# FFN's first half: GpSimd's second weight sum moved behind the next block's input-weight remainder

## The chip, the cores and the metric

The kernel runs on one core of a Trainium2 chip. The metric is the device time of one execution in microseconds. Its engines are TensorE (matrix products; in the profile PE, and PEld for its weight loads), VectorE (DVE), ScalarE (ACT), GpSimd (POOL) and SyncE (SP, which issues most transfers). Each engine works through its own queue in order and waits on semaphores for the others.

## The reference, cut to what matters

Three stages in a row: attention restricted to clusters of queries and keys, a feed-forward network (FFN) with a leaky activation, and a mixture of eight experts. The change is in the second:

```python
def _moe_ref(x, w_in, w_out, alpha) -> np.ndarray:
    h = x @ w_in
    g = np.maximum(h, 0.0) + alpha * np.minimum(h, 0.0)
    return (g @ w_out).astype(np.float32)
```

x is 1536 tokens x 512, w_in 512 x 2048, w_out 2048 x 512. The two weight matrices are given as 8-byte floating-point numbers, so the kernel has to make 4-byte ones of them.

## The kernel before

The FFN cuts the hidden width of 2048 into NF = 16 blocks f of 128 and the tokens into two halves gi of 768. The first half (gi = 0) runs through all 16 blocks, then the second half does. Block f's weights are 128 x 512 numbers of w_in and as many of w_out.

Each 4-byte operand is split into a rounded part and a remainder (`wh` and `wl` of the weights, `gh` and `gl` of the activations, `xh` and `xl` of x), and each product is made of three: high x high, and high x low both ways.

TensorE's order in a block of the first half: `product(c, i)` of line 672 for c = 0, 1 (two runs of 384 tokens) and i = 0, 1, 2: `wh` with xh, `wh` with xl, `wl` with xh, four matmuls each (line 677); then `second(0, f - 1)` (line 719), the previous block's activations times w_out, 18 matmuls (line 726).

After the three products of each c the activation follows: VectorE makes `gm` in two instructions from the PSUM tile h (lines 702 and 703), ScalarE rounds it to `gh` (line 705), VectorE subtracts to `gl` (line 707). Then `after(c)` (line 796) is issued:

- after c = 0: `split(f + 1, 0)` and `split(f, 1)`: the input weights of the next block and the output weights of this one. In each, ScalarE rounds to `wh` (line 648) and GpSimd subtracts to `wl` (line 649).
- after c = 1: `convert(f + 2)` (line 630): the 8-byte weights of block f + 2 become 4-byte ones in two halves, input weights and output weights. `word` (line 560) is a generator: ScalarE makes two operands (lines 569 and 570), VectorE takes three instructions (lines 571, 573, 575) in place in a tile `ct`, of which there are two buffers, and GpSimd adds at last (line 577). `convert` steps both halves in turn, so that each engine gets the first half's instruction and then the second's.

GpSimd's order in a block is therefore: the sum of the input weights, the sum of the output weights (both of line 577, issued by the block before), the subtraction for the next block's input weights, the subtraction for this block's output weights (both of line 649). In the texts below these four are A, B, X and Y. Blocks 2 to 13 convert; blocks 14 and 15 have nothing left to convert. Conversion of block 3 is issued ahead of block 2 (line 792), beside the end of the attention's normalisation on GpSimd (lines 412 to 415).

All order is that of the program's text; no planner moves anything.

Of the kernel before, what the change touches and what calls it, by code (L numbers as in the profile page):

```python
# [543 lines left out]
class Convert:  # L544
# [10 lines left out]
    def load(self, f):  # L555
        raw = self.slot(f)
        self.nc.sync.dma_start(out=raw[:, :DM].rearrange("p (k n) w -> p k (n w)", k=DM // P), in_=self.w_in[:, :, f])
        self.nc.sync.dma_start(out=raw[:, DM:].rearrange("p n w -> p (n w)"), in_=self.w_out[:, f])
# [53 lines left out]
def ffn(tc, A, cst, xs, xp, y1d, R, cv, W32, fw, ps_h, spare, more):  # L612
# [17 lines left out]
    def convert(f):  # L630

        if f < NF:
            gs = [cv.word(f, slice(q * DM, (q + 1) * DM), ck.tile([P, DM], I32, tag="ct", name="ct")) for q in range(2)]
            for _ in range(4):
                for g in gs:
                    next(g, None)

    ws, gs, over = {}, {}, {}

    def split(f, o, eng, gi=0):  # L640

        if o == 1 and gi == 1 and NF - TAIL <= f < NF - 2:
            wh, wl = over["xl"].pop(0), over["xl"].pop(0)
        else:
            wh = fw.tile([P, DM], F32R, tag=f"wh{o}", name=f"wh{o}")
            wl = fw.tile([P, DM], F32R, tag=f"wl{o}", name=f"wl{o}")
        w = W32(f)[:, o * DM:(o + 1) * DM]
        nc.scalar.copy(wh, w)
        eng.tensor_tensor(out=wl, in0=w, in1=wh.bitcast(F32), op=ALU.subtract)  # L649
        ws[f, o] = (wh, wl)  # L650
# [7 lines left out]
    def hidden(gi, f, eng, after, between=lambda: None):  # L658
        for _ in hiddens(gi, f, eng, after, between):
            pass  # L660

    def hiddens(gi, f, eng, after=lambda c: None, between=lambda: None, act=False):
# [17 lines left out]
        for c in range(2):  # L680
# [29 lines left out]
            if not act or f + c == 2:  # L710
                pay()
            after(c)
            if c == 1:
                gs[f] = (gh, gl)
# [4 lines left out]
    def second(gi, f, ns=range(3), ts=range(GT)):  # L719
        wh, wl = ws[f, 1]  # L720
        gh, gl = gs[f]
        for n, (a, w) in enumerate(((gh, wh), (gh, wl), (gl, wh))):
            for t in ts if n in ns else ():
                if f == 0 and n == 0:
                    ys[gi * GT + t] = ps_y.tile([P, DM], F32, tag="y", name="y")
                nc.tensor.matmul(ys[gi * GT + t], lhsT=a[:, t * P:(t + 1) * P], rhs=w,  # L726
                                 start=(f == 0 and n == 0), stop=(gi == 0 and f == NF - 1 and n == 2))
        if ns[-1] == 2 and ts[-1] == GT - 1:
            del ws[f, 1], gs[f]
# [60 lines left out]
    for f in (4, 5, 6):  # L790
        load(f)
    convert(3)
    second(0, 0)
    for f in range(2, NF):

        def after(c):
            if c == 0:
                split((f + 1) % NF, 0, nc.gpsimd)
                split(f, 1, nc.gpsimd)
            else:  # L800
                convert(f + 2)

        hidden(0, f, nc.vector, after)
        if f + 5 < NF:
            load(f + 5)
        second(0, f - 1)
# [742 lines left out]
def kernel(ctx, tc, A):  # L1549
# [164 lines left out]
    def begin():  # L1714
        ps_h = c2.enter_context(tc.tile_pool(name="ps_h", bufs=2, space=PSUM, side="right", reuse_waits="tile"))
        fw = c0.enter_context(tc.tile_pool(name="ffw", bufs=2, side="right", reuse_waits="tile"))
        return ffn(tc, A, cst, xs, xp, y1d, R, cv, lambda f: w32[f], fw, ps_h, spare, lambda *a: got.append(a) if a else more())
# [108 lines left out]
```

## Time and profile before

| | us |
|---|---|
| median of 3 runs | 718.74 |
| lowest, highest | 717.54, 721.0 |
| the profiled execution, device time | 718.92 |
| its span, first to last instruction | 717.1 |
| mean granted TensorE clock | 0.994 |
| busy: TensorE, weight loads | 699.9, 625.8 |
| busy: VectorE, ScalarE, GpSimd | 568.2, 472.1, 381.9 |

The profile is one execution. A page gives sums; views of the trace give groups of instructions, waits, and the instructions in order of time. Times in them are from the span's start, and the loop of the first half runs from about 263 to 385 us. Matmuls are pipelined, so that their busy times overlap and starts tell more than durations. In the order of time, instructions of one line that follow each other without a gap may stand merged as one row with their count (x2).

### The profile page before, as it was taken

How to read it: one execution, taken by the hardware profiler on the slowest of the kernel's cores; microseconds unless marked ns; L12 is line 12 of the kernel's file. 1: busy time of each engine (PE TensorE's matmuls, PEld its weight loads, DVE VectorE, ACT ScalarE, POOL GpSimd, SP SyncE). 2: the span in 40 equal slices, each digit the busy share in tenths (PEclk: the TensorE clock that was granted, in tenths of full speed). 3: DMA queues.
4: the chain of work that ended last, by engine and by line, in shares of the span. 5: the costliest groups of instructions: out<-in, count | busy, mean ns of one | idle time of the engine just before them, and what ended most of it. 6: DMA issues, size and time to landing. Idle time of an engine off the chain costs nothing.

```text
span 717.1 us, 11778 instructions
## 1 busy us (share of the span) xinstructions
PE 699.9 (98%) x4111; PEld 625.8 (87%) x4111; DVE 568.2 (79%) x1114; ACT 472.1 (66%) x905; POOL 381.9 (53%) x339
## 2 busy tenths in 40 slices
PE   8999999999999999999999999999999999999995
PEld 5998989989999899888889999999888989898884
DVE  6989988898989878788784989976468888785651
ACT  6889788888889954554545655556645867574640
POOL 4659779697896386666662000001025888884201
PEclk9999999999999999999999999999999999999998
DMA  7867666676765133333203600026444999996000
GB/s 204 213 160 177 133 166 157 156 173 127 169 164 123 41 115 122 133 138 136 119 1 122 188 0 1 1 64 202 147 149 139 385 367 320 353 352 262 33 10 25
DMA packets 43904, 108.42 MB, mean 151 GB/s; under 512 B 8698, under 2 KB 24522, under 8 KB 38464
## 3 DMA queue, kind: packets, MB, share of 16 engines
q1 hardware_dynamic: 36768, 67.03, 34.4%
q0 software_dynamic: 7072, 40.60, 15.3%
q8 instruction: 34, 0.56, 0.3%
q14 instruction: 30, 0.25, 0.1%
HBM read 74.78 MB, written 10.10 MB: 118 GB/s over the span
## 4 chain that ended last, share of the span: by engine, by line
PE 66%; DVE 8%; DMA 8%; ACT 6%; POOL 6%; issue 5%; POOLq 0%; SPq 0%; ACTq 0%; DVEq 0%
PE h L677 18%; PE y L726 16%; DMA raw<-in_wall_dram,wi 7%; PE yo L1210 5%; PE pt L342 4%; PE hw L1263 4%; PE h L1210 3%; PE s L308 2%; PE px L360 2%; DVE nm L324 2%; PE y L736 2%; ACT e L331 2%; PE s L311 2%; DVE etl L345 2%; PE px L362 2%
## 5 line engine op out<-in xcount | busy, mean ns | idle before, releaser
L345 DVE TENSOR_TENSOR etl<-pt,eth 128x384 fp32r<-128x384 f32 x192 | 101.9, 549 | 19.6 <-ACT eth L344 18.4
L344 ACT CAST eth<-pt 128x384 fp32r<-128x384 f32 x192 | 90.9, 485 | 19.4 <-PE pt L342 19.4
L1177 POOL DMA_INDIRECT xg<-y1d,gi x16 | 27.8, 1738 | 130.5 <-DVE gi L1026 113.8
L342 PE MATMUL pt<-ident,e 128*128 128x128 f32 x576 | 93.8, 272 | 0.3 <-ACT e L331 0.3
L331 ACT ACTIVATE e<-s,nm 128x768 f32<-128x768 f32 x96 | 87.4, 910 | 6.4 <-DVE nm L324 5.6
L324 DVE TENSOR_REDUCE nm<-s 128x1 f32<-128x768 f32 x96 | 90.5, 943 | 0.9 <-PE s L311 0.8
L705 ACT CAST gh<-gm 128x384 fp32r<-128x384 f32 x60 | 30.8, 513 | 81.8 <-DVE gm L703 58.5
L342 PEld LDWEIGHTS pt<-ident,e 128*128 128x128 f32 x576 | 73.6, 140 | 7.0 <-ACT e L331 0.6
L707 DVE TENSOR_TENSOR gl<-gm,gh 128x384 fp32r<-128x384 f32 x60 | 49.4, 824 | 25.7 <-ACT gh L705 25.7
L360 PE MATMUL px<-etl,vh 128*64 128x384 f32 (+1 forms) x192 | 65.5, 368 | 1.5 <-DVE etl L345 1.3
L308 PE MATMUL s<-AB 128*128 128x384 f32 x192 | 57.5, 381 | 2.5 <-ACT e L331 2.1
L577 POOL TENSOR_TENSOR pre<-ct,pre 128x512 int32<-128x512 int32 x26 | 37.2, 1451 | 35.8 <-DVE ct L575 35.8
L677 PE MATMUL h<-xh,wh 128*128 128x384 f32 x256 | 55.6, 338 | 0.6 <-DVE gm L700 0.4
L677 PE MATMUL h<-xh,wl 128*128 128x384 f32 x256 | 56.0, 339 | 0.0
L677 PE MATMUL h<-xl,wh 128*128 128x384 f32 x256 | 55.0, 336 | 0.0
L362 PE MATMUL px<-eth,vh 128*128 128x384 f32 x160 | 54.0, 337 | 0.0
L1545 DVE TENSOR_TENSOR wl<-raw,wh 128x2048 fp32r<-128x2048 f32 (+2 forms) x26 | 44.5, 1717 | 11.7 <-ACT wh L1541 11.7
L311 PE MATMUL s<-CD 128*128 128x384 f32 x192 | 49.3, 338 | 1.0 <-DVE CD L439 1.0
L677 PEld LDWEIGHTS h<-xh,wh 128*128 128x128 f32 x256 | 45.5, 188 | 3.3 <-DVE gm L700 0.5
L677 PEld LDWEIGHTS h<-xh,wl 128*128 128x128 f32 x256 | 44.6, 188 | 2.7 <-POOL wl L649 2.6
L677 PEld LDWEIGHTS h<-xl,wh 128*128 128x128 f32 x256 | 45.7, 188 | 0.0
L1541 ACT CAST wh<-raw 128x2048 fp32r<-128x2048 f32 (+2 forms) x26 | 37.4, 1444 | 10.6 <-PE yo L1210 10.6
(357 smaller groups left out, 1816.8 us busy)
## 6 DMA issues: line engine op xcount, KB each, us to landing
AB<-RL SPq DMA_DIRECT2D x31, 384.0 KB, 5.3
raw<-in_w_in_dram SPq DMA_DIRECT2D x16, 512.0 KB, 4.0
raw<-in_w_out_dram SPq DMA_DIRECT2D x16, 512.0 KB, 4.7
raw<-in_wall_dram SPq DMA_DIRECT2D x8, 1024.0 KB, 8.2
Tp<-in_qkT_dram SPq DMA_DIRECT2D x16, 384.0 KB, 4.1
CD<-RL SPq DMA_DIRECT2D x15, 384.0 KB, 6.9
raw<-in_wall_dram POOLq DMA_DIRECT2D x4, 1024.0 KB, 11.8
vt<-in_v_dram SPq DMA_DIRECT2D x8, 384.0 KB, 6.3
```

What stands on the lines that cost most here:

```text
L308: nc.tensor.matmul(s[:, u, :384], lhsT=AB[:, 0, t * P:(t + 1) * P], rhs=AB[:, 1, ks], start=True, stop=False)
L311: nc.tensor.matmul(s[:, u, :384], lhsT=CD[:, 0, t * P:(t + 1) * P], rhs=CD[:, 1, ks], start=False, stop=True)
L324: nc.vector.tensor_reduce(out=nm, in_=s[:, :, :384], axis=AX.XY, op=ALU.max, negate=True)
L331: nc.scalar.activation(e.rearrange("p (u c) -> p u c", u=2), s[:, :, :384], AF.Exp, bias=nm, accum_out=den[:, i % 3:i % 3 + 1])
L342: nc.tensor.transpose(pt[:, i2], e[:, kt * P:(kt + 1) * P], ident)
L344: nc.scalar.copy(eh, pt)
L345: lows[u] = lambda: nc.vector.tensor_tensor(out=etl[:, 3 * u:3 * u + 3, q * P:(q + 1) * P], in0=pt, in1=eh.bitcast(F32), op=ALU.subtract)
L360: nc.tensor.matmul(px[:m], lhsT=vh[:, kt, :m], rhs=etl[:, kt], start=False, stop=False)
L362: nc.tensor.matmul(px, lhsT=vh[:, kt, :], rhs=eth[:, kt], start=False, stop=(kt == NT - 1))
L677: nc.tensor.matmul(hs[c], lhsT=a[:, k * P:(k + 1) * P], rhs=x[:, k, c * HC:(c + 1) * HC], start=(k == 0 and i == 0), stop=(k == KD - 1 and ...
L726: nc.tensor.matmul(ys[gi * GT + t], lhsT=a[:, t * P:(t + 1) * P], rhs=w, start=(f == 0 and n == 0), stop=(gi == 0 and f == NF - 1 and n == 2))
L1210: nc.tensor.matmul(out, lhsT=l[:, k], rhs=r[:, k * DM:(k + 1) * DM], start=start and k == 0 and i == 0, stop=stop and k == 3 and i == len( ...
```

## The change

`convert` no longer takes the last step of the second half: the generator of that half is put aside in a list `sums`, with its GpSimd addition still to come. The next `after(0)` takes it between the two `split` calls. GpSimd's order in a block becomes A, X, B, Y. The order on every other engine is what it was, and no instruction is added or left out.

```diff
         if f < NF:
             gs = [cv.word(f, slice(q * DM, (q + 1) * DM), ck.tile([P, DM], I32, tag="ct", name="ct")) for q in range(2)]
-            for _ in range(4):
-                for g in gs:
+            for n in range(4):
+                for g in gs if n < 3 else gs[:1]:
                     next(g, None)
-
+            sums.append(gs[1])
+
+    sums = []
     ws, gs, over = {}, {}, {}
@@
         def after(c):
             if c == 0:
                 split((f + 1) % NF, 0, nc.gpsimd)
+                while sums:
+                    next(sums.pop(0), None)
                 split(f, 1, nc.gpsimd)
             else:
                 convert(f + 2)
```

## Rows read from the trace of the kernel before

**Rows 1.** The page: busy time by engine; granted TensorE clock in 40 slices.

```profile
PE 699.9 (98%) x4111; PEld 625.8 (87%) x4111; DVE 568.2 (79%) x1114; ACT 472.1 (66%) x905; POOL 381.9 (53%) x339
...
PEclk9999999999999999999999999999999999999998
```

**Rows 2.** Waits, 255 to 385 us: engine, line, awaited; total us, times, longest.

```profile
ACT gh L705 <- DVE gm L703: 58.5, 28, 4.0
POOL pre L577 <- DVE ct L575: 35.8, 13, 2.9
...
PEld h L677 <- POOL wl L649: 2.6, 10, 0.3
```

**Rows 3.** In order of time, TensorE: first products of blocks 2, 3, 7, 15 (start, duration).

```profile
263.50 0.68 PE L677 MATMUL h<-xh,wh 128*128 128x384 f32 x3
...
271.81 0.87 PE L677 MATMUL h<-xh,wh 128*128 128x384 f32 x4
...
305.31 0.69 PE L677 MATMUL h<-xh,wh 128*128 128x384 f32 x3
...
373.52 0.69 PE L677 MATMUL h<-xh,wh 128*128 128x384 f32 x3
```

**Rows 4.** In order of time, VectorE: one block (start, duration, [idle before]).

```profile
302.70 0.61 DVE L702 TENSOR_SCALAR gm<-h,alpha 128x384 f32<-128x384 f32 x1
...
304.56 1.04 DVE L707 TENSOR_TENSOR gl<-gm,gh 128x384 fp32r<-128x384 f32 x1 [0.66 <-ACT gh L705]
...
307.30 1.12 DVE L707 TENSOR_TENSOR gl<-gm,gh 128x384 fp32r<-128x384 f32 x1 [0.58 <-ACT gh L705]
308.33 0.41 DVE L571 TENSOR_SCALAR ct<-ct 128x512 f32<-128x512 f32 x1
308.99 0.43 DVE L571 TENSOR_SCALAR ct<-ct 128x512 f32<-128x512 f32 x1 [0.24 <-ACT ct L569]
309.33 0.76 DVE L573 TENSOR_SCALAR ct<-ct 128x512 int32<-128x512 int32 x2
310.00 1.29 DVE L575 SCALAR_TENSOR_TENSOR ct<-raw,ct 128x512 int32<-128x512 int32 x2
311.21 0.61 DVE L702 TENSOR_SCALAR gm<-h,alpha 128x384 f32<-128x384 f32 x1
```

**Rows 5.** The same block on GpSimd: B, X, Y, the next A.

```profile
303.89 1.29 POOL L577 TENSOR_TENSOR pre<-ct,pre 128x512 int32<-128x512 int32 x1
...
305.14 1.61 POOL L649 TENSOR_TENSOR wl<-pre,wh 128x512 fp32r<-128x512 f32 x1
...
306.71 1.29 POOL L649 TENSOR_TENSOR wl<-pre,wh 128x512 fp32r<-128x512 f32 x1
310.83 1.61 POOL L577 TENSOR_TENSOR pre<-ct,pre 128x512 int32<-128x512 int32 x1 [2.83 <-DVE ct L575]
```

**Rows 6.** The same block on ScalarE: `wh` for X; `ct` of the second half.

```profile
304.43 0.62 ACT L648 CAST wh<-pre 128x512 fp32r<-128x512 f32 x1
...
308.30 0.66 ACT L569 ACTIVATE ct<-raw 128x512 f32<-128x512 f32 x1
```

**Rows 7.** In order of time: VectorE and GpSimd before block 2; one L707 later.

```profile
263.69 0.99 DVE L707 TENSOR_TENSOR gl<-gm,gh 128x384 fp32r<-128x384 f32 x1 [0.58 <-ACT gh L705]
...
264.22 1.15 POOL L414 TENSOR_TENSOR xh<-xa,zero 128x384 fp32r<-128x384 f32 x1
...
264.60 1.05 DVE L571 TENSOR_SCALAR ct<-ct 128x512 f32<-128x512 f32 x1
...
265.57 1.24 DVE L571 TENSOR_SCALAR ct<-ct 128x512 f32<-128x512 f32 x1
...
389.36 0.56 DVE L707 TENSOR_TENSOR gl<-gm,gh 128x384 fp32r<-128x384 f32 x1 [0.58 <-ACT gh L705]
```

**Rows 8.** In order of time, VectorE: the first L702 of blocks 2 and 14.

```profile
268.61 0.61 DVE L702 TENSOR_SCALAR gm<-h,alpha 128x384 f32<-128x384 f32 x1
...
370.89 0.61 DVE L702 TENSOR_SCALAR gm<-h,alpha 128x384 f32<-128x384 f32 x1
```

## The prediction

> **What bounds the kernel now.** I read the page first: TensorE is busy for 98% of the span at a granted clock of 9 tenths or more in nearly every slice [rows 1], which would make any wait of TensorE worth its own length. So the next view is who waited for whom in the stretch of the loop that the change touches, 255 to 385 us [rows 2]. There TensorE's weight load waits for `wl` of line 649 for 2.6 us in all, ten times, the only row of any size in which TensorE waits. The starts of the first product in the blocks say the same from the other side [rows 3]: the first blocks come 271.81 - 263.50 = 8.31 us apart, and from block 2 to block 15 the 13 blocks take 373.52 - 263.50 = 110.02 us, 2.0 more than 13 x 8.31 = 108.0; block 15 waits once more, for 0.25. So all that TensorE loses in this loop is 2.0 to 2.6 us, and that is the most that a change of order can give here.
>
> The question is what keeps `wl` late in every block. VectorE's rows of one block answer it [rows 4]: from one first L702 to the next pass 311.21 - 302.70 = 8.51 us, and its three idle times (0.66, 0.58, 0.24 us) each end on ScalarE, which in turn had waited for VectorE's `gm` [rows 2]. None ends on TensorE. VectorE and ScalarE thus run round in a closed loop of 8.51 us, longer than TensorE's 8.31, and it is the same from block 2 on: the first L702 of block 2 and of block 14 lie (370.89 - 268.61) / 12 = 8.52 us apart [rows 8]. TensorE had some slack, lost 0.2 us of it in each block, and from block 6 on is held at the loop's pace. GpSimd is not full: it sits idle for 2.83 us a block until VectorE has made the next `ct` [rows 2, 5].
>
> What the loop's length is made of is the second thing to see. Both L707 take 1.04 and 1.12 us [rows 4], but the same instruction, form for form, takes 0.56 where GpSimd is idle [rows 7]. The first asks at 304.56, while GpSimd's second sum runs until 303.89 + 1.29 = 305.18 [rows 5], and ends 0.42 after that; the second asks at 307.30 during a subtraction that ends at 306.71 + 1.29 = 308.00, and ends 0.41 after it. The other way round, the subtraction of 305.14 takes 1.61 instead of 1.29 and ends 1.15 after the first L707 does (306.75 against 305.60). So the two engines don't work through such operands side by side: one holds and the other stands still.
>
> **The change part by part.** It adds and removes no instruction. Of each block's four GpSimd operations, sum A, sum B, subtraction X (`wl` of the next block's input weights), subtraction Y (`wl` of this block's output weights), it makes A, X, B, Y. No DMA moves, and no other queue is touched. Twelve blocks (2 to 13) also convert, and in them VectorE's L571 to L575 follow the second L707. I work one block through with the clock of [rows 4 to 6].
>
> X: it no longer waits for B, but it needs `wh`, which ScalarE delivers at 304.43 + 0.62 = 305.05 [rows 6]. X began at 305.14 and still does. The wait that the move takes away is replaced by ScalarE's, 0.1 us earlier; by this alone nearly nothing is won.
>
> First L707: GpSimd is now empty from 303.93 to 305.14, so L707 runs at once, 304.56 + 0.56 = 305.12 instead of 305.60: 0.48 us gained on the loop. X in turn stands still for nothing, and ends at 305.14 + 1.29 = 306.43 instead of 306.75, so `wl` is 0.32 earlier.
>
> Second L707: it asks 0.48 earlier, at 306.82. By then B runs, from 306.39 to 307.68 (GpSimd's operations follow each other 0.04 before the end, as 305.14 does on 305.18). L707 ends at 307.68 + 0.41 = 308.09 instead of 308.41: of the 0.48, 0.32 is left.
>
> Y: this is the place where it turns. Y stood before the second L707 in GpSimd's order and now stands behind it, beside the conversion. It asks from 307.64, gets its turn when L707 is done, and ends 1.15 after it, at 309.24. VectorE's next instruction, L571, asks at 308.01. The trace has this very sequence once, before block 2 [rows 7]: L707 is held, L414 of GpSimd stands behind it, L571 is issued next on VectorE; L414 goes first, and L571 ends 0.28 after it (264.22 + 1.15 = 265.37; 264.60 + 1.05 = 265.65), taking 1.05 us instead of 0.41 [rows 4]. So the first L571 ends at 309.24 + 0.28 = 309.52, where it ended at 308.74: 0.78 later. The idle time of 0.24 before the second L571 [rows 4] is swallowed: with nothing between them such instructions end 0.34 apart (308.99 to 309.33), so the second L571 ends near 309.52 + 0.34 = 309.86 instead of 309.42, 0.44 later. L573 and L575 follow back to back as before; Y is over, and A comes only after L575. The loop grows by 0.44 us, from 8.51 to 8.95.
>
> Of VectorE's arbitration I take this one row. Were L571 to go first, Y would slip in before the second L571 (308.45 + 1.15 = 309.60, + 0.28 = 309.88): the same 0.44. The lower bound is that Y never holds L571 (rival 1); the upper is the full 0.78 without the idle time swallowed, though nothing then says why the second L571 should wait, as its operand is ready by 308.5.
>
> The Trainium skill, page "SBUF — State Buffer", section "Who interferes with whom", has a rule that speaks against this change: a VectorE instruction with two SBUF inputs, or a one-input one in its two-port mode, and a GpSimd instruction exclude each other, and whichever issues first keeps the shared ports for the whole instruction. By it Y, issued before L571, goes first, which is what the row of L571 at 264.60 shows; it lowers the chance of rival 2 and changes no term.
>
> New wait: `ct` of the second half has two buffers in all, and ScalarE's next write of it (308.30 in [rows 6]; 307.82 with the shift of 0.48) must now come after B, which ends at 307.68. It fits by 0.14, and if it did not, the second L571 would still have some 0.9 us of cover. Sum B's result is first read a block later. Y's `wl` is read in the next block's second half of TensorE's work, over 4 us on. None of these cost.
>
> The sum: 12 turns from the first L702 of block 2 to that of block 14 x 0.44 = 5.3 us. There the L702 comes at 370.89 + 5.3 = 376.2; `wh` of block 15 follows 2.35 later (305.05 - 302.70) and the product 0.26 after that (305.31 for the block shown [rows 3]), near 378.8 instead of 373.52. Block 15's own wait for `wl` of 0.25 goes, since `wl` is there 3.73 after the L702, before TensorE asks. That leaves 5.0 us. Blocks 14 and 15 have no conversion behind them, VectorE has room there, and TensorE sets the pace again; the later stages are TensorE's own (98% busy) and shift as they are. Against the profiled execution's own 718.92 us that is 723.9; the median of the three runs is 0.18 lower, so 723.7. I take 723.8.
>
> **The rivals.** Rival 1, the move works: Y does not hold L571, because GpSimd and VectorE share better here than at 264.60. Then the loop shrinks by the 0.32 of the second L707 to 8.19, below TensorE's 8.31; TensorE sets the pace and gets back its 2.0 to 2.3 us: 716.6. For it speaks only that the face of the diff is this; against it speak both L571 beside GpSimd [rows 7], each of them held. A page's rule stands behind it: the Trainium skill, "Perfetto Trace Analysis", section "Identifying the Most-Contended Engine", would optimise the engine of highest occupancy first, TensorE by its weight loads. The loop on VectorE, which never waits for TensorE, is why I don't follow it here.
>
> Rival 2, nothing is measured: VectorE, once it has the turn, keeps it through L571 to L575 with Y standing behind. Then Y starts after the last L575 and pushes A, which runs into the next first L707 and takes back the 0.48 gained there; the rest of the turn is as before: 8.51 again, 718.7. Against it: L414 got its turn between two VectorE instructions that stood back to back.
>
> The point from which it decides is whether Y ends before or after the first L571 is issued, 308.01. By the rows it ends 1.2 us after.
>
> **How the numbers follow.** The forecast has a chance of 0.82, rival 1 0.08 and rival 2 0.08; 0.02 remain for something costlier, such as a lower granted clock once TensorE idles for 0.6 us in each block. The loop's growth is known to some 0.1 us, which over 12 turns is 1.2 us, and the runs of before lie between 717.54 and 721.0; so the forecast itself spans 721.3 to 726.0, and with that the range is filled. About 0.5%, 3.6 us, is what a measurement of this kernel can tell from no change; the bound of slower is then 722.3. Nine tenths of the forecast and the costlier rest lie above: slower 0.77; rival 2, most of rival 1 and the forecast's foot are within: 0.20; faster 0.03.
>
> **What would show it.** In the changed kernel X should still start right after `wh` and take 1.29; the first L707 should take 0.56, the second some 1.27, the first L571 some 1.5 with GpSimd's Y ending 0.28 before it; the first L702 should come every 8.95 us up to block 14; TensorE should wait for `wh` (line 648), not for `wl`, about 0.6 us a block, and the granted clock should stay. The prediction is wrong if L571 keeps 0.41, or if blocks stay at 8.5 us with L571 held, which would mean a cover that I have not seen.

## The result and the profile after

The changed kernel takes 723.51 us (median of 9 runs, 722.43 to 726.93); the kernel before takes 720.79 us over 9 runs taken beside it (717.54 to 721.01). The ratio is 1.0061 with a 95% interval of 1.0040 to 1.0083: slower by 0.6%, about 4.4 us. The ratio compares the means (719.79 and 724.19), since the runs of each kernel fall into two groups (717.5 to 718.9 and 720.8 to 721.0 before, 722.4 to 723.8 and 725.9 to 726.9 after) and the median of before lies in its upper group, that of the changed kernel in its lower one. The forecast was 723.8 and slower. Its chances counted a change of over 0.5% as one that a measurement can tell.

The page of the changed kernel, busy time by engine, and the granted clock:

```profile
PE 703.6 (97%) x4111; PEld 628.3 (87%) x4111; DVE 575.3 (79%) x1114; ACT 472.0 (65%) x905; POOL 382.0 (53%) x339
...
PEclk9999999999999999999999999999999999999999
```

Against [rows 1] VectorE is busy for 7.1 us more with the same 1114 instructions: some of them stand still while they count as busy (the rows of one block below show which). GpSimd's time is the same, and the granted clock did not fall (0.998 in the mean, against 0.994).

Who waited for whom in the loop, 255 to 390 us (engine, line, awaited; total us, times, longest). Two lines of code are added ahead of it, so line 649 is now 651, 677 is 679, 702 is 704 and 707 is 709:

```profile
POOL pre L577 <- DVE ct L575: 26.1, 13, 2.0
...
POOL wl L651 <- ACT wh L650: 16.6, 14, 1.2
PEld h L679 <- ACT wh L650: 8.6, 11, 0.8
...
PE h L679 <- ACT wh L650: 4.0, 11, 0.4
```

The wait of TensorE for `wl` in [rows 2] is gone. In its place TensorE waits for `wh`, 11 times where it waited 10 times for `wl`, and longer, and GpSimd waits for `wh` as well.

VectorE in one block, in order of time (start, duration, [idle before]); two neighbouring answers are put together:

```profile
306.59 0.61 DVE L704 TENSOR_SCALAR gm<-h,alpha 128x384 f32<-128x384 f32 x1
...
308.45 0.56 DVE L709 TENSOR_TENSOR gl<-gm,gh 128x384 fp32r<-128x384 f32 x1 [0.66 <-ACT gh L707]
...
310.71 1.27 DVE L709 TENSOR_TENSOR gl<-gm,gh 128x384 fp32r<-128x384 f32 x1 [0.58 <-ACT gh L707]
...
311.90 1.52 DVE L571 TENSOR_SCALAR ct<-ct 128x512 f32<-128x512 f32 x1
...
315.55 0.60 DVE L704 TENSOR_SCALAR gm<-h,alpha 128x384 f32<-128x384 f32 x1
```

GpSimd in the same block: X, B, Y, the next A; then ScalarE's `wh`, which X waits for, and TensorE's product from it.

```profile
309.01 1.29 POOL L651 TENSOR_TENSOR wl<-pre,wh 128x512 fp32r<-128x512 f32 x1 [1.19 <-ACT wh L650]
...
310.26 1.30 POOL L577 TENSOR_TENSOR pre<-ct,pre 128x512 int32<-128x512 int32 x1
...
311.53 1.61 POOL L651 TENSOR_TENSOR wl<-pre,wh 128x512 fp32r<-128x512 f32 x1
...
315.17 1.61 POOL L577 TENSOR_TENSOR pre<-ct,pre 128x512 int32<-128x512 int32 x1 [2.04 <-DVE ct L575]
```

```profile
308.32 0.61 ACT L650 CAST wh<-pre 128x512 fp32r<-128x512 f32 x1
...
308.99 0.79 PE L679 MATMUL h<-xh,wh 128*128 128x384 f32 x3 [0.35 <-ACT wh L650]
```

Set beside [rows 4, 5]: the first L709 fell from 1.04 to 0.56; the second grew from 1.12 to 1.27, ending at 311.98, 0.42 after B (311.56); Y is held by it from 311.53 and ends at 313.14, 1.16 after it; the first L571 grew from 0.41 to 1.52 and ends at 313.42, 0.28 after Y. In all 12 blocks that convert, L571 takes 1.51 to 1.52 and ends 0.28 to 0.29 after Y. One turn, from L704 to L704, is 315.55 - 306.59 = 8.96 us. X begins at 309.01, right behind `wh` (308.32 + 0.61 = 308.93) and, counted from the turn's first L704, at 2.42 us; before it was 305.14 - 302.70 = 2.44. GpSimd stands idle for 1.19 us ahead of X, time in which it used to do B.

Where the profiled times differ. First TensorE's first products of blocks 2 and 15; then TensorE's products near the start of the kernel, long before the change, in the changed kernel and in the kernel before, each from its own trace:

```profile
265.71 0.69 PE L679 MATMUL h<-xh,wh 128*128 128x384 f32 x3
...
380.66 0.96 PE L679 MATMUL h<-xh,wh 128*128 128x384 f32 x4 [0.35 <-ACT wh L650]
```

```profile
5.21 5.17 PE L188 MATMUL sim<-bd,Tp 128*128 128x32 f32 x24
```

```profile
4.99 2.83 PE L188 MATMUL sim<-bd,Tp 128*128 128x32 f32 x24
```

The profiled execution of the changed kernel took 725.97 us, its span is 724.2, 7.1 longer than before's. Of that, 265.71 - 263.50 = 2.2 us lie ahead of block 2, where both kernels run the same instructions; the first 24 small products there took 5.17 instead of 2.83 us (more on this at the end). From block 2 to block 15 it is 380.66 - 265.71 = 114.95 us against 110.02 [rows 3], 4.9 more. That is the change. What follows gives back no more than 0.1 us: 4.9 and 2.2 make 7.1. So the one profile overstates the change by nearly half, and in the experiments below I compare the turn, and where TensorE's pace is in question the stretch from block 2 to block 15, as well as the times.

### The profile page after: what moved, and what is told of

Read it like the earlier page. It is cut to its first block, busy times and chain, and to the rows that moved or that the text cites. A ratio compares the mean times of both kernels' runs of the same rounds, so it can differ in the third digit from the quotient of the medians.

```text
span 724.2 us, 11765 instructions
## 1 busy us (share of the span) xinstructions
PE 703.6 (97%) x4111; PEld 628.3 (87%) x4111; DVE 575.3 (79%) x1114; ACT 472.0 (65%) x905; POOL 382.0 (53%) x339
## 4 chain that ended last, share of the span: by engine, by line
PE 51%; DVE 20%; ACT 8%; DMA 8%; issue 6%; POOL 5%; SPq 1%; POOLq 0%; ACTq 0%; DVEq 0%
PE h L679 9%; PE y L728 7%; DMA raw<-in_wall_dram,wi 6%; PE yo L1214 6%; PE hw L1267 4%; PE pt L342 4%; DVE ct L571 3%; PE h L1214 3%; PE s L308 2%; DVE ct L575 2%; PE px L360 2%; PE sim L188 2%; DVE gl L709 2%; DVE nm L324 2%; PE y L738 2%
## 5 line engine op out<-in xcount | busy, mean ns | idle before, releaser
L707 ACT CAST gh<-gm 128x384 fp32r<-128x384 f32 x60 | 30.8, 513 | 86.7 <-DVE gm L705 63.5
L709 DVE TENSOR_TENSOR gl<-gm,gh 128x384 fp32r<-128x384 f32 x60 | 45.0, 751 | 25.7 <-ACT gh L707 25.7
L651 POOL TENSOR_TENSOR wl<-pre,wh 128x512 fp32r<-128x512 f32 x26 | 37.5, 1442 | 15.4 <-ACT wh L650 15.4
```

The costliest lines, as they stand in the source:

```text
L709: eng.tensor_tensor(out=gl[:, o], in0=m, in1=gh[:, o].bitcast(F32), op=ALU.subtract)
```

## The experiments

**The theories.** T1 is the prediction's: VectorE and ScalarE run a closed loop, and it grew because Y now stands behind the second `gl` subtraction and holds the conversion's first instruction. T2 is what the view of waits suggests at first sight: the wait for `wl` was replaced by a longer wait of GpSimd and TensorE for `wh`, and that wait is the loss. Turns below are from the first `gm` instruction (tensor_scalar, line 702 of the kernel before) of block 2 to that of block 14, divided by 12. The kernel before has 8.52 [rows 8], the changed one (378.27 - 270.79) / 12 = 8.96:

```profile
270.79 0.60 DVE L704 TENSOR_SCALAR gm<-h,alpha 128x384 f32<-128x384 f32 x1
...
378.27 0.60 DVE L704 TENSOR_SCALAR gm<-h,alpha 128x384 f32<-128x384 f32 x1
```

**Y made short and reading nothing.** Only in blocks 2 to 13:

```diff
-    def split(f, o, eng, gi=0):
+    def split(f, o, eng, gi=0, clear=False):
...
         nc.scalar.copy(wh, w)
-        eng.tensor_tensor(out=wl, in0=w, in1=wh.bitcast(F32), op=ALU.subtract)
+        if clear:
+            eng.memset(wl.bitcast(F32), 0.0)
+        else:
+            eng.tensor_tensor(out=wl, in0=w, in1=wh.bitcast(F32), op=ALU.subtract)
...
-                split(f, 1, nc.gpsimd)
+                split(f, 1, nc.gpsimd, clear=f < NF - 2)
```

> The changed kernel, with Y (the subtraction for the block's output weights in blocks 2 to 13) replaced by a memset of the same tile to zero on GpSimd; the low part of these weights is left out of the product. Order, waits and ScalarE's work stay. Theory T1 (the loop of VectorE and ScalarE grew because Y, behind the second gl subtraction, holds the first instruction of the conversion): a memset reads nothing and is short, so L571 is free or nearly so, VectorE's own loop falls to some 8.0 to 8.3 us and TensorE's 8.31 decides: first gm instruction of block 2 to that of block 14 at 8.31 a turn, TensorE hardly waits for wh, some 2 us faster than before (ratio 0.997). Rival T2 (the loss is the new wait of GpSimd and TensorE for ScalarE's wh, which took the place of the wait for wl): wh comes as in the changed kernel, so the turn stays 8.95 and the kernel stays some 4.8 us slower than before.

Measured: 718.43 us, ratio 0.9976 (0.9959 to 0.9992). Its VectorE, first `gm` of blocks 2, 12 and 14, and a second `gl` with the L571 behind it; then GpSimd's Y, and TensorE's first products of blocks 2 and 15:

```profile
270.32 0.60 DVE L707 TENSOR_SCALAR gm<-h,alpha 128x384 f32<-128x384 f32 x1
...
306.61 1.28 DVE L712 TENSOR_TENSOR gl<-gm,gh 128x384 fp32r<-128x384 f32 x1 [0.58 <-ACT gh L710]
...
307.82 0.41 DVE L571 TENSOR_SCALAR ct<-ct 128x512 f32<-128x512 f32 x1
...
350.73 0.61 DVE L707 TENSOR_SCALAR gm<-h,alpha 128x384 f32<-128x384 f32 x1
...
367.20 0.62 DVE L707 TENSOR_SCALAR gm<-h,alpha 128x384 f32<-128x384 f32 x1 [0.17 <-PE h L682]
```

```profile
307.40 0.55 POOL L652 MEMSET wl<- 128x512 f32 x1
```

```profile
265.22 0.87 PE L682 MATMUL h<-xh,wh 128*128 128x384 f32 x4
...
373.20 0.87 PE L682 MATMUL h<-xh,wh 128*128 128x384 f32 x4
```

B still holds the second `gl` (1.28), but L571 is back at 0.41. The turn is (367.20 - 270.32) / 12 = 8.07 us, below TensorE's 8.31, so that VectorE at last catches up with TensorE: the idle time of 0.17 that ends on PE is the first of its kind here. Its first ten turns, ahead of that, take (350.73 - 270.32) / 10 = 8.04 each. Blocks 2 to 15 take 373.20 - 265.22 = 107.98 us, 13 x 8.31, and no wait of TensorE is left in the stretch. `wh` and X were not touched; T2 expected 4.8 us more than before and falls. One size was off: I had TensorE's 8.31 for the turn, while VectorE, which had been behind, ran at its own 8.04 until it met TensorE. The memset differs from Y in two ways, it reads nothing and takes 0.55 us instead of 1.29 or more; which of the two frees L571 this run does not tell apart.

**Y a second time in the kernel before**, with the order A, B, X, Y:

```diff
                 split(f, 1, nc.gpsimd)
+                if f < NF - 2:
+                    wh, wl = ws[f, 1]
+                    nc.gpsimd.tensor_tensor(out=wl, in0=W32(f)[:, DM:], in1=wh.bitcast(F32), op=ALU.subtract)
             else:
```

> The kernel before, its order A, B, X, Y kept, with Y issued a second time right behind the first in blocks 2 to 13 (same result, one more GpSimd operation). T1: the second Y stands behind the second gl subtraction just as Y does in the changed kernel, without the 0.32 us that the change gains ahead of it: gl ends 308.41 on the clock of the block shown, the second Y 1.15 later, the first L571 at 309.84 (some 1.5 us long), the second at 310.18 instead of 309.42: turn 8.52 + 0.76 = 9.28 us, 9 us slower than before (ratio 1.0125). T2 (waiting for wh is what costs): here wl is late as before, wh is not awaited more, GpSimd has 2.8 us of idle time for an operation of 1.3: 8.52 a turn, no change.

Measured: 729.07 us, ratio 1.0129 (1.0104 to 1.0154). VectorE: first `gm` of blocks 2 and 14, and the pair in between; GpSimd's second Y:

```profile
269.50 0.61 DVE L702 TENSOR_SCALAR gm<-h,alpha 128x384 f32<-128x384 f32 x1
...
311.23 1.13 DVE L707 TENSOR_TENSOR gl<-gm,gh 128x384 fp32r<-128x384 f32 x1 [0.58 <-ACT gh L705]
...
312.28 1.51 DVE L571 TENSOR_SCALAR ct<-ct 128x512 f32<-128x512 f32 x1
...
380.92 0.60 DVE L702 TENSOR_SCALAR gm<-h,alpha 128x384 f32<-128x384 f32 x1
```

```profile
312.02 1.49 POOL L802 TENSOR_TENSOR wl<-pre,wh 128x512 fp32r<-128x512 f32 x1
```

The turn is (380.92 - 269.50) / 12 = 9.285, forecast 9.28. A GpSimd operation of 1.3 us, put into an idle time of 2.83 us, costs 0.76 us a turn, since in that idle time VectorE runs the conversion, and the operation holds its first instruction (1.51 us instead of 0.41). That is the cost of the place alone, without the 0.32 that the change gains ahead of it.

**B behind Y in the changed kernel**, order A, X, Y, B:

```diff
                 split((f + 1) % NF, 0, nc.gpsimd)
+                split(f, 1, nc.gpsimd)
                 while sums:
                     next(sums.pop(0), None)
-                split(f, 1, nc.gpsimd)
```

> The changed kernel with B behind Y: GpSimd's order A, X, Y, B. T1: the fourth operation, whichever it is, holds the first L571 by the same 0.78 us. But B is also the last reader of the ct that ScalarE writes next for the second half: in the changed kernel it is over 0.14 us before that write, here it ends at 309.24, so ScalarE writes 309.3 to 310.0 and the second L571 ends at 310.4 instead of 309.42: turn 8.52 + 1.0 = 9.5 us, 12 us slower than before (ratio 1.0165), the second L571 with an idle time of some 0.5 us before it that ends on ScalarE. Were the late buffer no matter, 8.95 and 4.8 us slower as the changed kernel. T2: wh and X are as in the changed kernel: 8.95.

Measured: 730.1 us, ratio 1.0159 (1.0133 to 1.0184). VectorE, then ScalarE:

```profile
267.12 0.60 DVE L704 TENSOR_SCALAR gm<-h,alpha 128x384 f32<-128x384 f32 x1
...
310.39 1.52 DVE L571 TENSOR_SCALAR ct<-ct 128x512 f32<-128x512 f32 x1
...
312.35 0.43 DVE L571 TENSOR_SCALAR ct<-ct 128x512 f32<-128x512 f32 x1 [0.44 <-ACT ct L569]
...
381.06 0.61 DVE L704 TENSOR_SCALAR gm<-h,alpha 128x384 f32<-128x384 f32 x1
```

```profile
311.65 0.66 ACT L569 ACTIVATE ct<-raw 128x512 f32<-128x512 f32 x1 [1.36 <-POOL pre L577]
```

The turn is (381.06 - 267.12) / 12 = 9.495, forecast 9.5. The first L571 is held by the same 1.52 as by Y: it is the place that counts, not which of the two stands there. On top of it the late B now holds back `ct`, which it does not in the changed kernel.

**Both Abs first, in the kernel before.** This takes 0.33 us out of VectorE's loop and touches neither GpSimd's order nor `wh`:

```diff
         nc.scalar.activation(tf, hi.bitcast(F32), AF.Abs)
-        nc.scalar.activation(w, top, AF.Copy, scale=2.0 ** -13)
         nc.vector.tensor_scalar(out=tf, in0=tf, scalar1=MIN_HI, scalar2=None, op0=ALU.max)
         yield
+        nc.scalar.activation(w, top, AF.Copy, scale=2.0 ** -13)
         nc.vector.tensor_scalar(out=t, in0=t, scalar1=3, scalar2=0x3FFFFFF8, op0=ALU.logical_shift_left, op1=ALU.bitwise_and)
```

> The kernel before, GpSimd's order kept, with ScalarE's four conversion instructions in another order: both Abs (L569) first, then both copies (L570), instead of Abs, copy, Abs, copy. T1 (VectorE's and ScalarE's closed loop sets the pace and TensorE is held by it): the idle time of 0.24 us before the second L571 goes, the second L571 starts 0.33 us earlier, VectorE's own turn becomes 8.19, below TensorE's 8.31: turn 8.31, TensorE waits for wl no more, 2.0 to 2.3 us faster than before (ratio 0.997). T2 (TensorE's wait for wl is GpSimd's order): neither GpSimd's order nor the wait for wh changes, so wl comes as late: 8.52 a turn, no change.

Measured: 716.26 us (10 runs), ratio 0.9964 (0.9950 to 0.9978): faster than both kernels. VectorE, then TensorE's first products of blocks 2 and 15:

```profile
267.40 0.60 DVE L702 TENSOR_SCALAR gm<-h,alpha 128x384 f32<-128x384 f32 x1
...
312.95 1.13 DVE L707 TENSOR_TENSOR gl<-gm,gh 128x384 fp32r<-128x384 f32 x1 [0.58 <-ACT gh L705]
314.00 0.75 DVE L570 TENSOR_SCALAR ct<-ct 128x512 f32<-128x512 f32 x2
...
365.77 0.61 DVE L702 TENSOR_SCALAR gm<-h,alpha 128x384 f32<-128x384 f32 x1
```

```profile
262.29 0.69 PE L677 MATMUL h<-xh,wh 128*128 128x384 f32 x3
...
370.28 0.87 PE L677 MATMUL h<-xh,wh 128*128 128x384 f32 x4
```

The two instructions of L571 (here line 570) stand back to back, the turn is (365.77 - 267.40) / 12 = 8.20, VectorE's own as in y_clear and not the 8.31 that I had written, blocks 2 to 15 take 370.28 - 262.29 = 107.99 us, and the wait for `wl` is gone although X comes where it came, counted from the turn's first `gm` (310.79 - 308.36 = 2.43, before 2.44). The 2 us that the change was after were to be had on VectorE and ScalarE.

**Both Abs first, in the changed kernel**, the same edit:

> The changed kernel with ScalarE's conversion in the other order (both Abs of L569 first, then both copies). It tests one step of the sum, that the idle time of 0.24 us before the second L571 is already swallowed in the changed kernel. T1: the second L571 follows the held first one and does not wait for ScalarE, so an earlier Abs gives nothing: turn 8.95 as in the changed kernel, 4.8 us slower than before (ratio 1.0065). Rival T1b (the idle time of 0.24 is still there and the cost of Y adds to it): the turn falls by 0.33 to 8.63, 1.2 us slower than before (ratio 1.002). T2 (wait for wh): 8.95 too, since wh is not touched.

Measured: 725.99 us, ratio 1.0088 (1.0063 to 1.0112), forecast 1.0065. VectorE:

```profile
270.39 0.60 DVE L704 TENSOR_SCALAR gm<-h,alpha 128x384 f32<-128x384 f32 x1
...
311.47 1.85 DVE L570 TENSOR_SCALAR ct<-ct 128x512 f32<-128x512 f32 x2
...
377.83 0.61 DVE L704 TENSOR_SCALAR gm<-h,alpha 128x384 f32<-128x384 f32 x1
```

The turn is (377.83 - 270.39) / 12 = 8.95. The edit that gives some 0.33 us a turn in the kernel before gives nothing here: the idle time of 0.24 had already gone under the held instruction. By itself this run is a weaker test than it was meant to be, since the late B now holds ScalarE's second Abs back for 0.35 us and it comes only 0.12 earlier, counted from `gl` (311.16 - 310.28 = 0.88 against 311.71 - 310.71 = 1.00). But the changed kernel's own rows say the same:

```profile
311.90 1.85 DVE L571 TENSOR_SCALAR ct<-ct 128x512 f32<-128x512 f32 x2
```

```profile
311.71 0.65 ACT L569 ACTIVATE ct<-raw 128x512 f32<-128x512 f32 x1
```

The second L571's operand is ready at 312.36, 1.06 before the held first one ends at 313.42, and the pair ends at 313.75, 7.16 into the turn instead of 309.42 - 302.70 = 6.72. This is the step of the sum that makes 0.44 out of 0.78.

## Why the prediction was right, step by step

- **X gains next to nothing by itself.** It starts 2.42 us into the turn instead of 2.44, on `wh`, and takes 1.29 where 1.29 was forecast.
- **The first `gl` is free.** 0.56, as forecast.
- **The second `gl` is held by B.** 1.27, as forecast.
- **Y goes before L571 and holds it.** 1.52 against 1.5, Y 0.28 ahead of its end. The single earlier instance in [rows 7] was enough to know the order of the two; it came out the same in each of the 12 blocks. By the Trainium skill's rule that the prediction weighed ("SBUF — State Buffer", "Who interferes with whom") the one that issues first keeps the shared ports; the trace agrees, with Y starting at 311.53 and L571 at 311.90. Here Y got them although both stood waiting behind the second `gl`, which ended at 311.98.
- **The idle time is swallowed.** The turn is 8.96 against 8.95, and the rows under abs_after show the swallowing.
- **The sum over 12 turns** was 5.3 us; measured 12 x (8.957 - 8.524) = 5.2. The way from there to TensorE was sized a little high: I let the product start 0.26 us after `wh`, as in the kernel before, where it also had to end the products ahead of it. In the changed kernel `wh` ends at 308.93 and the product starts at 308.99. So block 15's product came 4.9 us later and not 5.3; of the 0.25 that its wait for `wl` was to give back, some 0.1 came, and what reaches the end is 4.8 to 4.9 instead of 5.0.
- **The clock** stayed, though TensorE now stands for some 0.65 us in each block (8.96 - 8.31).

The runs decide against both rivals. Rival 1 needed L571 to be free beside Y; it is only in y_clear, where Y is a short memset. Rival 2 needed VectorE to keep its turn; it didn't in any block. The ratio of 1.0061 is 4.4 us, and its interval, 2.9 to 6.0 us, takes in the 4.9 of the trace. That the median of 723.51 came so near to 723.8 is in part luck: the mean of its nine runs is 724.19, and the sum started from 718.92, where the nine runs of the kernel before have a mean of 719.79. The growth of the turn, 0.44 forecast and 0.43 measured, is not luck.

## What to carry to other kernels

Before moving work to let one wait end sooner, look whether the engine that waits is held by a loop of other engines. Here three idle times that end on each other's work, and none on the bottleneck, said that the loop had to be shortened, and an exchange of two ScalarE instructions did it (8.52 to 8.20 us a turn), while earlier `wl` did not. Idle time of GpSimd is not free time when VectorE runs instructions that GpSimd's hold, here the `gl` subtraction (0.56 us alone, 1.27 beside B) and L571 (0.41, beside Y 1.52): 1.3 us put into 2.8 us of idleness cost 0.76 us a turn. And when an operation is taken out of the way of one instruction, write down beside which instruction it lands.

## What the runs showed that was not expected

GpSimd's memset of 128x512, which reads nothing, took 0.55 us from 307.40, while the second `gl` was in its own turn (B ended at 307.48 and `gl` at 307.89): `gl` ended 0.41 after B, as it did with the subtraction behind it (0.42), and the memset did not take the 1.61 of the subtraction in that place.

The kernel's first microseconds differ between executions of the same instructions. The first 24 products of line 188 took 2.77 to 3.28 us in four traces (before, y_twice, b_last, abs_before) and 5.17 in the other three. In before and y_twice the granted clock also stood at 0.51 and 0.50, its level of 1.2 GHz, from 9 to 12 us; it fell in the microsecond from 8 to 9, of which TensorE was busy for 0.46 and 0.55 us. In the other five it was 1.00 there. The first product of block 2, ahead of which all the kernels are the same but for the two exchanged ScalarE instructions, came at 262.02 and 262.29 us in the two traces with neither (b_last, abs_before), at 263.50 and 264.40 in the two with the low clock, and at 265.22 to 265.71 in the three with the long products. Such 3.7 us would be most of the scatter of one kernel's times (717.48 to 722.1 us in 21 runs of before), but that the scatter comes from there is not shown, since each kernel has one trace; the 2.2 us between the two profiled executions are near half of the change that was to be measured. What decides it was not tried.
